# Weights in 28 to 32 KiB runs per partition through a ring of five 32 KiB slots, with block transposes on VectorE, in a decode layer

## The chip, the cores and the metric

The kernel runs on one core of a Trainium2 chip. The metric is the device time of one execution in microseconds (us), as the median over several executions. KB and KiB are 1024 bytes here, MB a million. An execution counts as slow when it is over 1.5% above the fastest of the same kernel. Anything within 2% counts as the same. The sums below use ratios to runs of the kernel before on the same chip.

## The reference, cut to what matters

It is one decode step (one token) of a transformer layer for a batch of 4: layer norm, attention over the last 2048 cached keys (32 query heads, 4 key/value heads, head size 128), output projection, residual, layer norm, a SwiGLU block with 3584 hidden units, residual.

```python
x  = A_x                                          # [4, 1, 1024]
q  = layernorm(x) @ wq                            # wq [1024, 4096]
p  = softmax(q . k[:, :, -2048:] * 128**-0.5)     # k, v: [4, 4, 8192, 128]
h  = x + (p . v[:, :, -2048:]) @ wo               # wo [4096, 1024]
n  = layernorm(h)
h2 = h + (silu(n @ w1) * (n @ w3)) @ w2           # w1, w3 [1024, 3584], w2 [3584, 1024]
```

Everything is bf16. The inputs that must be read once come to 55.58 MB: wq, k, v and wo are 8.39 MB each, and w1, w3, w2 are 7.34 MB each. There are only four tokens, so each weight is used very little: this is a program that streams memory.

## The kernel before

All large inputs pass through one ring of ten slots of 16 KiB per partition, in the order wq, k, v, wo, w1, w3, w2. A slot is refilled when the matmuls that read it are done. How a weight is laid over the 128 partitions sets how many contiguous bytes (a run) go to one partition in one DMA.

```python
stream = ctx.enter_context(tc.tile_pool(name="stream", bufs=10))
...
wq_v = A_wq.rearrange("(p kc) n -> p kc n", kc=KC)             # 2 rows = 16 KB per run
wo_v = A_wo.rearrange("(h4 p r) n -> p h4 r n", p=P, r=RPO)    # 4 rows =  8 KB per run
w2_v = B_w2.rearrange("(j p i) n -> p j i n", p=P, i=IF)       # 7 rows = 14 KB per run
...
    in_=(B_w1, B_w3)[i][c * KPC * P : (c + 1) * KPC * P, :].rearrange("(p r) f -> p r f", r=KPC)  # 14 KB
...
    in_=A_v_cache[b, :, Sk - W : Sk, :].rearrange("g (p j) d -> p g j d", j=NK)   # v: 4 KB per run
```

K is read in 16 KB runs. The layout of a weight also fixes where the activations that meet it must stand. So the kernel before turns them with PE (TensorE, the matrix engine; here a matmul against the identity or a selection matrix) and copies the result out of PSUM, the memory that matmuls write to:

```python
for r in range(RPO):                     # attention output, for wo
    nc.tensor.matmul(o4_ps[:, r, :, :, :], lhsT=sel[:, r, :, :], rhs=OT_sb[:], start=True, stop=True)
for hh in range(RPO):
    nc.vector.tensor_copy(out=o4[hh * MP : (hh + 1) * MP, :, :, :]..., in_=o4_ps[hh * MP : ...])
...
for i in range(IF):                      # SwiGLU product, for w2
    nc.tensor.transpose(out=hg_ps[:, i, :], in_=hg_v[:, i, :], identity=ident[:])
nc.vector.tensor_copy(out=hgT[:, :, :, :, 0], in_=hg_ps[:]...)
```

Of the kernel before, what the change touches and what calls it, by code (L numbers as in the profile page):

```python
# [10 lines left out]
P = 128  # L11
# [3 lines left out]
BF16 = mybir.dt.bfloat16  # L15
# [4 lines left out]
def kernel(  # L20
# [38 lines left out]
    stream = ctx.enter_context(tc.tile_pool(name="stream", bufs=10))  # L59
# [8 lines left out]
    QD = P // JG  # L68
    CQ = Hq * Dh // JG
# [3 lines left out]
    IF = CF // P  # L73
    PK = P // Hkv
    JK = W // PK
    assert CQ == REP * Dh and CF == IF * P and HF <= 512


    KPC = 2
    HPC = 8  # L80
    RPO = 4
    assert CG == KPC * P
    wq_v = A_wq.rearrange("(p kc) n -> p kc n", kc=KC)
    wo_v = A_wo.rearrange("(h4 p r) n -> p h4 r n", p=P, r=RPO)
    w2_v = B_w2.rearrange("(j p i) n -> p j i n", p=P, i=IF)

    def load_wq(c):
        wq_t = stream.tile([P, KPC, Hq * Dh], BF16, tag="s")
        nc.sync.dma_start(out=wq_t[:], in_=wq_v[:, c * KPC : (c + 1) * KPC, :])
        return wq_t  # L90

    def load_k(b):

        k_t = stream.tile([P, JK * Dh], BF16, tag="s")
        nc.sync.dma_start(
            out=k_t[:],
            in_=A_k_cache[b, :, Sk - W : Sk, :].rearrange("g (pp j) d -> pp g (j d)", pp=PK),
        )
        return k_t

    def load_v(b):
        v_t = stream.tile([P, Hkv, NK, Dh], BF16, tag="s")
        nc.sync.dma_start(
            out=v_t[:],
            in_=A_v_cache[b, :, Sk - W : Sk, :].rearrange("g (p j) d -> p g j d", j=NK),
        )
        return v_t

    def load_wo(c):
        wo_t = stream.tile([P, HPC // RPO, RPO, D], BF16, tag="s")  # L110
        nc.sync.dma_start(
            out=wo_t[:], in_=wo_v[:, c * (HPC // RPO) : (c + 1) * (HPC // RPO), :, :]
        )
        return wo_t

    def load_w13(i, c):
        w13_t = stream.tile([P, KPC, F], BF16, tag="s")
        nc.sync.dma_start(
            out=w13_t[:],
            in_=(B_w1, B_w3)[i][c * KPC * P : (c + 1) * KPC * P, :].rearrange(  # L120
                "(p r) f -> p r f", r=KPC
            ),
        )
        return w13_t

    def load_w2(j, pieces):
        w2_t = stream.tile([P, IF, D], BF16, tag="s")
        i = 0
        for n in pieces:
            nc.sync.dma_start(out=w2_t[:, i : i + n, :], in_=w2_v[:, j, i : i + n, :])  # L130
            i += n
        return w2_t

    plan = (
        [("wq", load_wq, (c,)) for c in range(KC // KPC)]
        + [("k", load_k, (b,)) for b in range(B)]
        + [("v", load_v, (b,)) for b in range(B)]
        + [("wo", load_wo, (c,)) for c in range(Hq // HPC)]
        + [("w1", load_w13, (0, c)) for c in range(KC // KPC)]
        + [("w3", load_w13, (1, c)) for c in range(KC // KPC)]  # L140
        + [("w2", load_w2, (j, [IF] if j < JG - 1 else [4, 2, 1])) for j in range(JG)]
    )
# [3 lines left out]
    def load_next(n=1):  # L146
        for _ in range(n):
            if cursor[0] < len(plan):
                kind, f, args = plan[cursor[0]]
                loaded.setdefault(kind, []).append(f(*args))  # L150
                cursor[0] += 1
# [3 lines left out]
    load_next(10)  # L155
# [8 lines left out]
    for j in range(JG):  # L164
        nc.scalar.dma_start(
            out=x_q[QD * j : QD * j + B, :], in_=x_flat[:, j * CG : (j + 1) * CG]
        )
# [20 lines left out]
    for kc in range(KC):  # L188
# [9 lines left out]
    nc.vector.memset(qz[:], 0.0)  # L198

    RS = QD // B  # L200
    spread = const.tile([P, JG, B, RS], FP32)
    nc.vector.memset(spread[:], 0.0)
    nc.vector.tensor_copy(
        out=spread[:, :, :, 0], in_=ident[:].rearrange("p (j x) -> p j x", j=JG)[:, :, :B]
    )
    hgT = act.tile([P, IF, JG, B, RS], BF16)
    nc.gpsimd.memset(hgT[:], 0.0)

    sel = const.tile([P, RPO, RPO, P // RPO], BF16)
    ident_r = ident[:].rearrange("p (m r) -> p r m", r=RPO)  # L210
    for hh in range(RPO):
        nc.vector.tensor_copy(out=sel[:, :, hh, :], in_=ident_r)
# [12 lines left out]
    for kc in range(KC):  # L225
        wq_t = loaded["wq"][kc // KPC]
        for hf in range(CQ // 512):
            for g in range(JG):
# [4 lines left out]
                    rhs=wq_t[:, kc % KPC, c0 : c0 + 512],  # L233
# [3 lines left out]
        if kc % KPC == KPC - 1:  # L237
            load_next()
# [33 lines left out]
    for u, (b, n) in enumerate(units):  # L272
        k_v = loaded["k"][b][:].rearrange("p (j d) -> p j d", d=Dh)
# [15 lines left out]
        if n == NSB - 1:  # L289
            load_next()  # L290
# [35 lines left out]
    for b in range(B):  # L326
# [10 lines left out]
        load_next()  # L337
    OT_sb = act.tile([P, Hq, B], BF16)
    nc.vector.tensor_copy(out=OT_sb[:].rearrange("p h b -> p b h"), in_=OT_ps[:])

    o4_ps = psA.tile([P, RPO, Hq // RPO, RPO, B], FP32, tag="kt3")
    for r in range(RPO):
        nc.tensor.matmul(o4_ps[:, r, :, :, :], lhsT=sel[:, r, :, :], rhs=OT_sb[:], start=True, stop=True)
    o4 = act.tile([P, Hq // RPO, RPO, B], BF16)
    MP = P // RPO
# [16 lines left out]
    for h4 in range(Hq // RPO):  # L362
# [10 lines left out]
        if h4 % (HPC // RPO) == HPC // RPO - 1:  # L373
            load_next()
# [124 lines left out]
```

## Time and profile before

| | before |
|---|---|
| time, median of the first three runs | 139.99 us |
| span in the profile | 138.0 us |
| busy: PE, VectorE (DVE), ScalarE (ACT) | 53%, 27%, 21% |
| data queue q1: bytes, packets, share of 16 engines' span | 55.58 MB, 6388, 95.4% |

These are lines of the page of the kernel before: the span, the busy time of each engine, the DMA rows (busy tenths and GB/s in 40 slices of the span), the data queue (packets, MB, share), and the chain of waits by engine.

```profile
span 138.0 us, 2358 instructions
...
PE 73.8 (53%) x1057; PEld 44.6 (32%) x1057; DVE 37.7 (27%) x72; ACT 29.1 (21%) x28; POOL 1.5 (1%) x7
...
DMA  5999999999999999999999999999999999999940
GB/s 159 447 410 432 437 423 432 446 418 423 446 401 415 414 420 424 415 431 424 427 432 420 427 434 432 424 436 428 433 424 432 432 420 440 420 445 414 415 197 2
...
q1 hardware_dynamic: 6388, 55.58, 95.4%
...
DMA 61%; PE 22%; ACT 10%; DVE 2%; issue 2%; ACTq 0%
```
The DMA row reads 9 (90% or more) in all slices but the first and the last two, while no compute engine is busy for much over half of the span. So the 16 DMA engines set the time. The chain of waits agrees. Its end, with start, length and what it was, is this:

```profile
...
76.67 27.64 DMA w_t<-in_B_w_dram
104.33 29.25 DMA w_t<-in_B_w_dram
133.62 0.62 PE y_ps L457 x6
134.25 0.43 PE y_ps L457 x3
134.71 0.42 DVE res L467
```
At 134.25 the last four matmuls begin (the chain counts three of them). After them come one VectorE copy (0.42 us) and the output DMA.

### The profile page before, as it was taken

What the parts mean: (1) busy time and instruction counts of PE and PEld (TensorE: products, weight loads), DVE (VectorE), ACT (ScalarE), POOL (GpSimd) and SP (SyncE); (2) the same over time, 40 slices, a digit from 0 to 9 for tenths busy, and PEclk for the clock granted to TensorE, in tenths of its full rate; (3) what the DMA queues carried; (4) which work ended last, traced back from release to release, by engine and by line L of the source; (5) the groups of instructions that cost most, each with busy time, mean ns of one, the idle gap of its engine ahead of it and who ended that gap; (6) DMA issues with size and microseconds to landing.
All of it is one profiled execution on the core that took longest, in us unless ns stands there. A gap on an engine that the chain in (4) does not pass through costs nothing.

```text
span 138.0 us, 2358 instructions
## 1 busy us (share of the span) xinstructions
PE 73.8 (53%) x1057; PEld 44.6 (32%) x1057; DVE 37.7 (27%) x72; ACT 29.1 (21%) x28; POOL 1.5 (1%) x7
## 2 busy tenths in 40 slices
PE   0152354499898989600596649382244422654370
PEld 0110011296565656300586637120011110233330
DVE  6710000242342525450410171510008930310001
ACT  2200000125373737449450000000041000000000
POOL 4000000000000000000000000000000000000000
PEclk9999999999999999975555557975555555555555
DMA  5999999999999999999999999999999999999940
GB/s 159 447 410 432 437 423 432 446 418 423 446 401 415 414 420 424 415 431 424 427 432 420 427 434 432 424 436 428 433 424 432 432 420 440 420 445 414 415 197 2
DMA packets 6437, 55.74 MB, mean 404 GB/s; under 512 B 504, under 2 KB 536, under 8 KB 2844
## 3 DMA queue, kind: packets, MB, share of 16 engines
q1 hardware_dynamic: 6388, 55.58, 95.4%
q8 instruction: 8, 0.13, 0.3%
q10 hardware_dynamic: 40, 0.02, 0.1%
q14 instruction: 1, 0.01, 0.0%
HBM read 55.59 MB, written 0.01 MB: 403 GB/s over the span
## 4 chain that ended last, share of the span: by engine, by line
DMA 61%; PE 22%; ACT 10%; DVE 2%; issue 2%; ACTq 0%
DMA w_t<-in_B_w_dram 41%; DMA k_t<-in_A_k_cache_dram 14%; PE kt_ps L278 11%; DMA wq_t<-in_A_wq_dram 5%; ACT kT L284 5%; PE scores_ps L263 5%; PE OT_ps L330 4%; ACT Pm L302 3%; DVE rmax L297 2%; PE pt_ps L316 1%; ACT L302 1%; PE y_ps L457 1%; ACT PT_sb L322 0%; DVE res L467 0%; DVE Dm L309 0%
## 5 line engine op out<-in xcount | busy, mean ns | idle before, releaser
L278 PE MATMUL kt_ps<-ident,k_t 128*128 128x128 bf16 x256 | 18.8, 237 | 1.0 <-DMA k_t<-in_A_k_cache_dram 1.0
L284 ACT COPY kT<-kt_ps 128x1024 bf16<-128x1024 bf16 x16 | 15.9, 1013 | 15.4 <-PE kt_ps L278 15.4
L278 PEld LDWEIGHTS <-k_t 128*128 128x128 bf16 x256 | 16.6, 107 | 6.1 <-issue 4.9
L282 DVE COPY kT<-kt_ps 128x1024 bf16<-128x1024 bf16 x16 | 11.1, 692 | 18.5 <-PE kt_ps L278 18.5
L230 PE MATMUL q_ps<-wq_t,xnT 128*4 128x512 bf16 x64 | 7.5, 621 | 11.2 <-DMA wq_t<-in_A_wq_dram 11.2
L424 PE MATMUL u_ps<-w_t,hnT 128*4 128x448 bf16 x64 | 6.7, 567 | 10.4 <-DMA w_t<-in_B_w_dram 10.4
L424 PEld LDWEIGHTS <-hnT 128*4 128x4 bf16 x128 | 3.8, 104 | 23.9 <-issue 23.2
L263 PE MATMUL scores_ps<-kT,qz 128*32 128x512 bf16 x64 | 9.9, 610 | 3.0 <-ACT kT L284 3.0
L457 PE MATMUL y_ps<-w_t,hgT 128*32 128x256 bf16 x112 | 7.1, 414 | 6.6 <-DMA w_t<-in_B_w_dram 5.8
L424 PE MATMUL g_ps<-w_t,hnT 128*4 128x448 bf16 x64 | 5.9, 516 | 5.4 <-DMA w_t<-in_B_w_dram 5.1
L330 PE MATMUL OT_ps<-PT_sb,v_t 128*128 128x8 bf16 x256 | 7.4, 168 | 2.0 <-issue 1.8
L330 PEld LDWEIGHTS <-v_t 128*128 128x128 bf16 x256 | 7.3, 104 | 2.2 <-issue 2.1
L457 PEld LDWEIGHTS <-hgT 128*32 128x32 bf16 x112 | 4.5, 135 | 9.2 <-issue 7.3
L230 PEld LDWEIGHTS <-xnT 128*4 128x4 bf16 x64 | 2.0, 106 | 15.9 <-issue 15.5
L316 PE MATMUL pt_ps<-Dm,Pm 128*128 128x128 bf16 x16 | 1.9, 311 | 9.3 <-DVE Dm L309 9.3
L366 PE MATMUL y_ps<-wo_t,o 128*4 128x256 bf16 x128 | 5.3, 344 | 1.7 <-DVE y_ps L356 1.7
L437 DVE RECIPROCAL eg<-eg 128x896 f32<-128x896 f32 x1 | 5.8, 5752 | 0.0
L240 DVE TENSOR_SCALAR q_sb<-q_ps 128x512 bf16<-128x512 f32 x1 | 0.7, 692 | 17.1 <-PE q_ps L230 17.1
L241 ACT ACTIVATE q_sb<-q_ps 128x512 bf16<-128x512 f32 x1 | 0.6, 597 | 20.9 <-DVE q_sb L240 20.9
L316 PEld LDWEIGHTS <-Pm 128*128 128x128 bf16 x16 | 1.6, 146 | 9.8 <-ACT Pm L302 9.8
L302 ACT ACTIVATE Pm<-scores_ps,nmax 128x2048 bf16<-128x2048 f32 x1 | 4.8, 4783 | 0.0
L366 PEld LDWEIGHTS <-o 128*4 128x4 bf16 x128 | 3.5, 105 | 3.5 <-DVE y_ps L356 2.0
(74 smaller groups left out, 40.5 us busy)
## 6 DMA issues: line engine op xcount, KB each, us to landing
w_t<-in_B_w_dram SPq DMA_DIRECT2D x11, 1792.0 KB, 33.3
wq_t<-in_A_wq_dram SPq DMA_DIRECT2D x4, 2048.0 KB, 11.8
k_t<-in_A_k_cache_dram SPq DMA_DIRECT2D x4, 2048.0 KB, 19.5
v_t<-in_A_v_cache_dram SPq DMA_DIRECT2D x4, 2048.0 KB, 38.4
wo_t<-in_A_wo_dram SPq DMA_DIRECT2D x4, 2048.0 KB, 22.9
w_t<-in_B_w_dram SPq DMA_DIRECT2D x1, 1024.0 KB
w_t<-in_B_w_dram SPq DMA_DIRECT2D x1, 512.0 KB, 29.2
w_t<-in_B_w_dram SPq DMA_DIRECT2D x1, 256.0 KB
```

What stands on the lines that cost most here:

```text
L230: nc.tensor.matmul(q_ps[QD * g : QD * g + B, hf * 512 : (hf + 1) * 512], lhsT=xnT[:, kc, :], rhs=wq_t[:, kc % KPC, c0 : c0 + 512], start=( ...
L263: nc.tensor.matmul(scores_ps[QD * g : QD * (g + 1), n * 512 : (n + 1) * 512], lhsT=qz[:, b, g * QD : (g + 1) * QD], rhs=kT_v[:, g, :, :], ...
L278: nc.tensor.transpose(out=kt_ps[:, jj, :], in_=k_v[:, n * NJ + t * TB + jj, :], identity=ident[:])
L282: nc.vector.tensor_copy(out=kT[:, t * TB : (t + 1) * TB, :], in_=kt_ps[:])
L284: nc.scalar.copy(out=kT[:, t * TB : (t + 1) * TB, :], in_=kt_ps[:])
L302: nc.scalar.activation(out=Pm[:].rearrange("q (c jq) -> q jq c", jq=NSB), in_=scores_ps[:].rearrange("q (jq c) -> q jq c", jq=NSB), func=A ...
L316: nc.tensor.matmul(pt_ps[:, jj, :], lhsT=Pm[:, (jb * JPB + jj) * P : (jb * JPB + jj + 1) * P], rhs=Dm[:], start=True, stop=True)
L330: nc.tensor.matmul(OT_ps[:, b, g * REP : (g + 1) * REP], lhsT=v_t[:, g, j, :], rhs=PT_sb[:, j, g * QD + b * REP : g * QD + (b + 1) * REP], ...
L366: nc.tensor.matmul(y_ps[QD * j : QD * j + B, :], lhsT=o4[:, h4, r, :], rhs=wo_t[:, h4 % (HPC // RPO), r, j * CG : (j + 1) * CG], start=(h4 ...
L424: nc.tensor.matmul(out_ps[QD * j : QD * j + B, hf, :HF], lhsT=hnT[:, k2, r, :], rhs=w_t[:, r, c0 : c0 + HF], start=(k2 == 0 and r == 0), s ...
L437: nc.vector.reciprocal(out=eg[:], in_=eg[:])
L457: nc.tensor.matmul(y2_ps[QD * j : QD * (j + 1), :], lhsT=hgT[:, i, jf, :, :].rearrange("p b s -> p (b s)"), rhs=w2_t[:, i, j * CG : (j + 1 ...
```

## The change

The intent is fewer and longer runs: a "p-major" layout, in which partition p holds consecutive rows of a weight, gives 32 KB per run for wq and wo, 28 KB for w1 and w3, and 32 KB for w2, in five slots of 32 KiB. The first slot of wq is still filled by two pieces of 16 KB, and the last slot of w2 by pieces of 10, 8, 4 and 2 KB. The new layout puts the activations just so that a 32x32 block transpose on VectorE can turn them, in place of PE transposes and strided copies. The core of the diff, with cuts:

```diff
-    stream = ctx.enter_context(tc.tile_pool(name="stream", bufs=10))
+    stream = ctx.enter_context(tc.tile_pool(name="stream", bufs=5))
...
-    wo_v = A_wo.rearrange("(h4 p r) n -> p h4 r n", p=P, r=RPO)
-    w2_v = B_w2.rearrange("(j p i) n -> p j i n", p=P, i=IF)
+    SLOT = 16384
+    RQ = 4
+    RO = 16
+    BS = 2
+    wq_v = A_wq.rearrange("(p i) n -> p (i n)", i=KC)
+    wo_v = A_wo.rearrange("(p i) n -> p (i n)", i=IO)
+    w1_v = B_w1.rearrange("(p i) n -> p (i n)", i=KC)
+    w3_v = B_w3.rearrange("(p i) n -> p (i n)", i=KC)
+    w2_v = B_w2.rearrange("(p i) n -> p (i n)", i=IF)
+    def load_rows(src, n, r0, pieces):
+        t = stream.tile([P, SLOT], BF16, tag="s")
+        i = 0
+        for m in pieces:
+            nc.sync.dma_start(
+                out=t[:, i * n : (i + m) * n], in_=src[:, (r0 + i) * n : (r0 + i + m) * n]
+            )
+            i += m
+        return [t[:, k * n : (k + 1) * n] for k in range(i)]
...
+        [("wq", load_rows, (wq_v, N_Q, c, [2, 2] if c == 0 else [4])) for c in range(0, KC, RQ)]
...                                         # k and v: two batches share a slot, runs as before
+        + [("wo", load_rows, (wo_v, D, c, [RO])) for c in range(0, IO, RO)]
+        + [("w1", load_rows, (w1_v, N_F, c, [RQ])) for c in range(0, KC, RQ)]
+        + [("w3", load_rows, (w3_v, N_F, c, [RQ])) for c in range(0, KC, RQ)]
+        + [("w2", load_rows, (w2_v, D, 0, [16])), ("w2", load_rows, (w2_v, D, 16, [5, 4, 2, 1]))]
...
-    for r in range(RPO):
-        nc.tensor.matmul(o4_ps[:, r, :, :, :], lhsT=sel[:, r, :, :], rhs=OT_sb[:], start=True, stop=True)
-    ... (four strided copies)
+    nc.vector.transpose(out=oT[:].rearrange("p b i -> p (b i)"), in_=OT_sb[:].rearrange("p b h -> p (b h)"))
+    nc.tensor.matmul(o4_ps[:], lhsT=perm[:], rhs=oT[:], start=True, stop=True)
...
-        nc.tensor.transpose(out=hg_ps[:, i, :], in_=hg_v[:, i, :], identity=ident[:])
+    nc.vector.transpose(
+        out=hgT[:].rearrange("p i x -> p (i x)"),
+        in_=hg[:].rearrange("q s c -> q (s c)").rearrange("q (c i) -> q i c", i=IF),
+    )
```

The transposes for w1/w3 (hn) change in the same way. The memsets of three PSUM tiles go, since now all rows of them are written.

More of the change, by code (lines that the diff above doesn't have):

```diff
@@ L68 @@
     QD = P // JG
+    RS = QD // B
     CQ = Hq * Dh // JG
@@ L72 @@
     HF = CF // 2
-    IF = CF // P
+    IO = Hq * Dh // P
+    IF = F // P
     PK = P // Hkv
     JK = W // PK
-    assert CQ == REP * Dh and CF == IF * P and HF <= 512
-    KPC = 2
-    HPC = 8
-    RPO = 4
-    assert CG == KPC * P
-    wq_v = A_wq.rearrange("(p kc) n -> p kc n", kc=KC)
-    wo_v = A_wo.rearrange("(h4 p r) n -> p h4 r n", p=P, r=RPO)
-    w2_v = B_w2.rearrange("(j p i) n -> p j i n", p=P, i=IF)
-    def load_wq(c):
-        wq_t = stream.tile([P, KPC, Hq * Dh], BF16, tag="s")
-        nc.sync.dma_start(out=wq_t[:], in_=wq_v[:, c * KPC : (c + 1) * KPC, :])
-        return wq_t
@@ L92, in load_k @@
-    def load_k(b):
-        k_t = stream.tile([P, JK * Dh], BF16, tag="s")
-        nc.sync.dma_start(
-            out=k_t[:],
-            in_=A_k_cache[b, :, Sk - W : Sk, :].rearrange("g (pp j) d -> pp g (j d)", pp=PK),
-        )
-        return k_t
-    def load_v(b):
-        v_t = stream.tile([P, Hkv, NK, Dh], BF16, tag="s")
-        nc.sync.dma_start(
-            out=v_t[:],
-            in_=A_v_cache[b, :, Sk - W : Sk, :].rearrange("g (p j) d -> p g j d", j=NK),
-        )
-        return v_t
@@ L109, in load_wo @@
-    def load_wo(c):
-        wo_t = stream.tile([P, HPC // RPO, RPO, D], BF16, tag="s")
-        nc.sync.dma_start(
-            out=wo_t[:], in_=wo_v[:, c * (HPC // RPO) : (c + 1) * (HPC // RPO), :, :]
-        )
-        return wo_t
-    def load_w13(i, c):
-        w13_t = stream.tile([P, KPC, F], BF16, tag="s")
-        nc.sync.dma_start(
-            out=w13_t[:],
-            in_=(B_w1, B_w3)[i][c * KPC * P : (c + 1) * KPC * P, :].rearrange(
-                "(p r) f -> p r f", r=KPC
-            ),
-        )
-        return w13_t
@@ L126, in load_w2 @@
-    def load_w2(j, pieces):
-        w2_t = stream.tile([P, IF, D], BF16, tag="s")
-        i = 0
-        for n in pieces:
-            nc.sync.dma_start(out=w2_t[:, i : i + n, :], in_=w2_v[:, j, i : i + n, :])
-            i += n
-        return w2_t
-    plan = (
-        [("wq", load_wq, (c,)) for c in range(KC // KPC)]
-        + [("k", load_k, (b,)) for b in range(B)]
-        + [("v", load_v, (b,)) for b in range(B)]
-        + [("wo", load_wo, (c,)) for c in range(Hq // HPC)]
-        + [("w1", load_w13, (0, c)) for c in range(KC // KPC)]
-        + [("w3", load_w13, (1, c)) for c in range(KC // KPC)]
-        + [("w2", load_w2, (j, [IF] if j < JG - 1 else [4, 2, 1])) for j in range(JG)]
+    assert CQ == REP * Dh and HF <= 512 and CG == QD * KC and CF == QD * IF and IO == QD == Hq
@@ new lines, in load_k @@
+    def load_k(b):
+        t = stream.tile([P, SLOT], BF16, tag="s")
+        out = []
+        for k in range(BS):
+            v = t[:, k * JK * Dh : (k + 1) * JK * Dh]
+            nc.sync.dma_start(
+                out=v,
+                in_=A_k_cache[b + k, :, Sk - W : Sk, :].rearrange("g (pp j) d -> pp g (j d)", pp=PK),
+            )
+            out.append(v)
+        return out
+    def load_v(b):
+        t = stream.tile([P, SLOT], BF16, tag="s")
+        out = []
+        for k in range(BS):
+            v = t[:, k * JK * Dh : (k + 1) * JK * Dh].rearrange("p (g j d) -> p g j d", g=Hkv, d=Dh)
+            nc.sync.dma_start(
+                out=v,
+                in_=A_v_cache[b + k, :, Sk - W : Sk, :].rearrange("g (p j) d -> p g j d", j=NK),
+            )
+            out.append(v)
+        return out
@@ new lines @@
+    N_Q, N_F = Hq * Dh, F
+    plan = (
+        [("wq", load_rows, (wq_v, N_Q, c, [2, 2] if c == 0 else [4])) for c in range(0, KC, RQ)]
+        + [("k", load_k, (b,)) for b in range(0, B, BS)]
+        + [("v", load_v, (b,)) for b in range(0, B, BS)]
+        + [("wo", load_rows, (wo_v, D, c, [RO])) for c in range(0, IO, RO)]
+        + [("w1", load_rows, (w1_v, N_F, c, [RQ])) for c in range(0, KC, RQ)]
+        + [("w3", load_rows, (w3_v, N_F, c, [RQ])) for c in range(0, KC, RQ)]
+        + [("w2", load_rows, (w2_v, D, 0, [16])), ("w2", load_rows, (w2_v, D, 16, [5, 4, 2, 1]))]
@@ L149, in load_next @@
                 kind, f, args = plan[cursor[0]]
-                loaded.setdefault(kind, []).append(f(*args))
+                loaded.setdefault(kind, []).extend(f(*args))
                 cursor[0] += 1
@@ L154 @@
     nc.scalar.dma_start(out=x_sb[:], in_=x_flat)
-    load_next(10)
+    load_next(5)
     ident = const.tile([P, P], BF16)
@@ L165 @@
         nc.scalar.dma_start(
-            out=x_q[QD * j : QD * j + B, :], in_=x_flat[:, j * CG : (j + 1) * CG]
+            out=x_q[QD * j : QD * (j + 1) : RS, :], in_=x_flat[:, j * CG : (j + 1) * CG]
         )
@@ L198 @@
     nc.vector.memset(qz[:], 0.0)
-    RS = QD // B
-    spread = const.tile([P, JG, B, RS], FP32)
-    nc.vector.memset(spread[:], 0.0)
+    ident_f = const.tile([P, P], FP32)
+    nc.vector.tensor_copy(out=ident_f[:], in_=ident[:])
+    perm = const.tile([P, P], BF16)
     nc.vector.tensor_copy(
-        out=spread[:, :, :, 0], in_=ident[:].rearrange("p (j x) -> p j x", j=JG)[:, :, :B]
-    )
-    hgT = act.tile([P, IF, JG, B, RS], BF16)
-    nc.gpsimd.memset(hgT[:], 0.0)
-    sel = const.tile([P, RPO, RPO, P // RPO], BF16)
-    ident_r = ident[:].rearrange("p (m r) -> p r m", r=RPO)
-    for hh in range(RPO):
-        nc.vector.tensor_copy(out=sel[:, :, hh, :], in_=ident_r)
+        out=perm[:].rearrange("p (h dq) -> p h dq", dq=JG),
+        in_=ident[:].rearrange("p (dq h) -> p h dq", dq=JG),
+    )
+    o4 = act.tile([P, IO, B, RS], BF16)
+    nc.gpsimd.memset(o4[:], 0.0)
     same = const.tile([P, JG, QD], FP32)
@@ L225 @@
     for kc in range(KC):
-        wq_t = loaded["wq"][kc // KPC]
+        wq_t = loaded["wq"][kc]
         for hf in range(CQ // 512):
@@ L232 @@
                     lhsT=xnT[:, kc, :],
-                    rhs=wq_t[:, kc % KPC, c0 : c0 + 512],
+                    rhs=wq_t[:, c0 : c0 + 512],
                     start=(kc == 0),
@@ L236 @@
                 )
-        if kc % KPC == KPC - 1:
+        if kc % RQ == RQ - 1:
             load_next()
@@ L272 @@
     for u, (b, n) in enumerate(units):
-        k_v = loaded["k"][b][:].rearrange("p (j d) -> p j d", d=Dh)
+        k_v = loaded["k"][b].rearrange("p (j d) -> p j d", d=Dh)
         kT = ktpool.tile([P, NJ, P], BF16, tag="kT")
@@ L288 @@
             emit_scores(u - 1)
-        if n == NSB - 1:
+        if n == NSB - 1 and b % BS == BS - 1:
             load_next()
@@ L336 @@
                 )
-        load_next()
-    OT_sb = act.tile([P, Hq, B], BF16)
-    nc.vector.tensor_copy(out=OT_sb[:].rearrange("p h b -> p b h"), in_=OT_ps[:])
-    o4_ps = psA.tile([P, RPO, Hq // RPO, RPO, B], FP32, tag="kt3")
-    for r in range(RPO):
-        nc.tensor.matmul(o4_ps[:, r, :, :, :], lhsT=sel[:, r, :, :], rhs=OT_sb[:], start=True, stop=True)
-    o4 = act.tile([P, Hq // RPO, RPO, B], BF16)
-    MP = P // RPO
-    for hh in range(RPO):
-        nc.vector.tensor_copy(
-            out=o4[hh * MP : (hh + 1) * MP, :, :, :].rearrange("p h r b -> p r h b"),
-            in_=o4_ps[hh * MP : (hh + 1) * MP, :, :, hh, :],
-        )
+        if b % BS == BS - 1:
+            load_next()
+    OT_sb = act.tile([P, B, Hq], BF16)
+    nc.vector.tensor_copy(out=OT_sb[:], in_=OT_ps[:])
+    oT = act.tile([P, B, IO], BF16)
+    nc.vector.transpose(out=oT[:].rearrange("p b i -> p (b i)"), in_=OT_sb[:].rearrange("p b h -> p (b h)"))
+    o4_ps = psA.tile([P, B, IO], FP32, tag="kt3")
+    nc.tensor.matmul(o4_ps[:], lhsT=perm[:], rhs=oT[:], start=True, stop=True)
+    nc.vector.tensor_copy(out=o4[:, :, :, 0], in_=o4_ps[:].rearrange("p b i -> p i b"))
     psA_cm.__exit__(None, None, None)
@@ L355 @@
     y_ps = psB.tile([P, CG], FP32, tag="y")
-    nc.vector.memset(y_ps[:], 0.0)
     y2_ps = psB.tile([P, CG], FP32, tag="y2")
     g_ps = psB.tile([P, 2, 512], FP32, tag="g")
-    nc.vector.memset(g_ps[:], 0.0)
     u_ps = psB.tile([P, 2, 512], FP32, tag="u")
-    nc.vector.memset(u_ps[:], 0.0)
-    for h4 in range(Hq // RPO):
-        wo_t = loaded["wo"][h4 * RPO // HPC]
-        for r in range(RPO):
-            for j in range(JG):
-                nc.tensor.matmul(
-                    y_ps[QD * j : QD * j + B, :],
-                    lhsT=o4[:, h4, r, :],
-                    rhs=wo_t[:, h4 % (HPC // RPO), r, j * CG : (j + 1) * CG],
-                    start=(h4 == 0 and r == 0),
-                    stop=(h4 == Hq // RPO - 1 and r == RPO - 1),
-                )
-        if h4 % (HPC // RPO) == HPC // RPO - 1:
+    for i in range(IO):
+        for j in range(JG):
+            nc.tensor.matmul(
+                y_ps[QD * j : QD * (j + 1), :],
+                lhsT=o4[:, i, :, :].rearrange("p b s -> p (b s)"),
+                rhs=loaded["wo"][i][:, j * CG : (j + 1) * CG],
+                start=(i == 0),
+                stop=(i == IO - 1),
+            )
+        if i % RO == RO - 1:
             load_next()
@@ L400 @@
     )
-    hn_ps = psB.tile([P, KPC, P], BF16, tag="tp")
-    hn_v = hn[:].rearrange("q (p r) -> q r p", r=KPC)
-    for r in range(KPC):
-        nc.tensor.transpose(out=hn_ps[:, r, :], in_=hn_v[:, r, :], identity=ident[:])
-    hnT = act.tile([P, JG, KPC, B], BF16)
-    nc.vector.tensor_copy(
-        out=hnT[:], in_=hn_ps[:].rearrange("p r (j x) -> p j r x", j=JG)[:, :, :, :B]
-    )
-    nc.tensor.matmul(
-        y2_ps[:], lhsT=spread[:].rearrange("p j b s -> p (j b s)"), rhs=h1[:],
-        start=True, stop=False, skip_group_check=True,
-    )
+    hnT = act.tile([P, KC, QD], BF16)
+    nc.vector.transpose(
+        out=hnT[:].rearrange("p k x -> p (k x)"), in_=hn[:].rearrange("q (c k) -> q k c", k=KC)
+    )
+    nc.tensor.matmul(y2_ps[:], lhsT=ident_f[:], rhs=h1[:], start=True, stop=False, skip_group_check=True)
     def gate_up(kind, out_ps):
-        for k2 in range(KC // KPC):
-            w_t = loaded[kind][k2]
-            for r in range(KPC):
-                for hf in range(2):
-                    for j in range(JG):
-                        c0 = j * CF + hf * HF
-                        nc.tensor.matmul(
-                            out_ps[QD * j : QD * j + B, hf, :HF],
-                            lhsT=hnT[:, k2, r, :],
-                            rhs=w_t[:, r, c0 : c0 + HF],
-                            start=(k2 == 0 and r == 0),
-                            stop=(k2 == KC // KPC - 1 and r == KPC - 1),
-                        )
-            load_next()
+        for k in range(KC):
+            for hf in range(2):
+                for j in range(JG):
+                    c0 = j * CF + hf * HF
+                    nc.tensor.matmul(
+                        out_ps[QD * j : QD * (j + 1), hf, :HF],
+                        lhsT=hnT[:, k, :],
+                        rhs=loaded[kind][k][:, c0 : c0 + HF],
+                        start=(k == 0),
+                        stop=(k == KC - 1),
+                    )
+            if k % RQ == RQ - 1:
+                load_next()
     gate_up("w1", g_ps)
@@ L442 @@
     nc.vector.tensor_tensor(out=hg[:], in0=u_ps[:, :, :HF], in1=gs[:], op=ALU.mult)
-    hg_ps = psB.tile([P, IF, P], BF16, tag="tp")
-    hg_v = hg[:].rearrange("q s c -> q (s c)").rearrange("q (p i) -> q i p", i=IF)
-    for i in range(IF):
-        nc.tensor.transpose(out=hg_ps[:, i, :], in_=hg_v[:, i, :], identity=ident[:])
-    nc.vector.tensor_copy(
-        out=hgT[:, :, :, :, 0], in_=hg_ps[:].rearrange("p i (j x) -> p i j x", j=JG)[:, :, :, :B]
-    )
-    for jf in range(JG):
-        w2_t = loaded["w2"][jf]
-        for i in range(IF):
-            for j in range(JG):
-                nc.tensor.matmul(
-                    y2_ps[QD * j : QD * (j + 1), :],
-                    lhsT=hgT[:, i, jf, :, :].rearrange("p b s -> p (b s)"),
-                    rhs=w2_t[:, i, j * CG : (j + 1) * CG],
-                    start=False,
-                    stop=(jf == JG - 1 and i == IF - 1),
-                    skip_group_check=True,
-                )
+    hgT = act.tile([P, IF, QD], BF16)
+    nc.vector.transpose(
+        out=hgT[:].rearrange("p i x -> p (i x)"),
+        in_=hg[:].rearrange("q s c -> q (s c)").rearrange("q (c i) -> q i c", i=IF),
+    )
+    for i in range(IF):
+        for j in range(JG):
+            nc.tensor.matmul(
+                y2_ps[QD * j : QD * (j + 1), :],
+                lhsT=hgT[:, i, :],
+                rhs=loaded["w2"][i][:, j * CG : (j + 1) * CG],
+                start=False,
+                stop=(i == IF - 1),
+                skip_group_check=True,
+            )
     res = act.tile([P, CG], BF16)
```

## The prediction

> **What bounds the kernel now.** The loads. The page's DMA queue lines give queue q1 55.58 MB in 6388 packets and 95.4% of 16 engines' span (131.7 of 138.0 us); in the 40 slices DMA reads 9 from the second slice to the end, about 425 GB/s. PE is busy 53%, DVE 27%, ACT 21%. The chain of waits is 61% DMA, and its last 57 us are w1/w3/w2 transfers: last landing 133.58, then 1.1 us of matmuls, 0.42 us of DVE, and the output DMA. The PE/ACT stretch of the chain (K transposes to OT, 27.6 to 76.7 us) is not the bound: DMA stays full behind it.
>
> **What the change does, costed.** The trace's DMA packet records have one size per contiguous run: 2 KB 84 ns, 4 KB 159, 8 KB 309, 14 KB 535, 16 KB 611. That is about 9 ns plus bytes/27.2 per ns. [...] By the fit (estimates) a 32 KB packet takes 1213 ns, 28 KB 1063, 10 KB 385. Per engine: wq 19.55 to 19.48 us, wo 19.78 to 19.41, w1+w3 34.24 to 34.02, w2 17.26 to 17.20. Sum: 0.7 us less DMA time. K and V are unchanged.
>
> Removed compute: four o copies (1.19 us), selection matmuls, y/g/u memsets (2.1 us), hg and hn transposes through PE with their copies. Added: three DVE block transposes (128, 256, 896 columns[...]). OT to first wo matmul (78.4 to 81.2) should fall from 2.8 to about 1.6 us. All of it hides behind the DMA.
>
> Moved: loads wait for 32 KiB slots. Capacity is the same 160 KiB, look-ahead four slots of 9.7 us instead of nine of 4.85. The second wq slot lands whole, so PE has 32 q matmuls after it (3.8 instead of 1.9 us), and K work starts about 1.3 us later. When each slot is freed, against when the queue would run dry (estimates from landings): first w1 slot issued near 59, needed by 81; second near 74, by 90; w3 near 79 and 84, by 98 and 107; w2 near 87 and 94, by 115 and 125. Never dry. The tail: w2's last pieces of 5, 4, 2, 1 rows end as before with four matmuls after the last landing; 16 rows (64 matmuls at 60 ns, 3.9 us) fit in the 7.2 us before. hgT is ready about 4 us before the first w2 slot lands.
>
> The larger pitch of the weight rows (56 or 64 KB per partition) could hurt HBM; [...] Here wq already has 64 KB pitch and runs at 431 GB/s, so I expect none.
>
> **Predicted:** 139.2 us, 8 in 10 within 138.3 to 140.2. Faster by over 2%: 0.05; within 2%: 0.90; slower by over 2%: 0.05.
>
> **What would show it.** q1 near 4,700 packets, sizes up to 32 KB at about 1213 ns; DMA 9 in all slices; wo and w1/w3/w2 phases at 430 to 435 GB/s instead of 418 to 433; last landing near 132.8; the same four-matmul tail.
>
> **What would make it wrong.** A gap in the DMA slices, where a slot is freed too late; 32 KB runs split or slower than the fit; HBM slower at the new pitch (would show as longer packets); a block transpose with strided input of several us, which would put hgT behind the w2 landing.

## More of the kernel before

Next, three stretches of the kernel before in the windows view. The columns are the stretch, its length, the busy time (and count) of each engine, the granted clock, the DMA share and the rate. The first stretch is V (4 KB runs), the second wo (8 KB), the third mostly w1 and w3 (14 KB).

```profile
core 0: us, PE busy (x) PEld busy (x) DVE busy (x) ACT busy (x) POOL busy (x), PEclk, DMA share, GB/s
43.00:60.00 17.00, 13.08 (x164) 8.44 (x163) 7.57 (x9) 8.10 (x9) 0.00 (x0) 1.00 1.02 418
64.00:79.00 15.00, 9.21 (x274) 8.99 (x275) 2.25 (x5) 5.05 (x5) 0.00 (x0) 0.50 1.01 427
84.00:114.00 30.00, 14.27 (x198) 5.76 (x191) 10.05 (x14) 2.50 (x3) 0.00 (x0) 0.61 1.01 430
...
```

The rate grows with the run: 418, 427, 430 GB/s. The DMA share is the summed duration of the packet records divided by 16 engines' time. It is 1.01 to 1.02, over 1.

## The result, and the profile after

The changed kernel took 139.39 us (median of 6 runs, 139.26 to 139.57), the kernel before 139.88 us in the same comparison (6 runs). The ratio is 0.9965, with an interval from 0.9952 to 0.9978. It is the mean time of the one kernel's fast runs over that of the other's of the same rounds, so not quite the ratio of the medians. The change is a gain of 0.49 us (139.88 x 0.0035), clear of noise, and far within "the same" at 2%. Five rounds more, later, gave 0.9967. The prediction was 139.2, within 138.3 to 140.2. That range holds the time of the kernel before as well (139.88), so that the number alone says little about the mechanism; the experiments have to show that.

The same lines of the page, of the changed kernel:

```profile
span 137.4 us, 2307 instructions
...
PE 71.2 (52%) x1045; PEld 45.2 (33%) x1045; DVE 36.3 (26%) x63; ACT 29.0 (21%) x28; POOL 1.6 (1%) x7
...
DMA  5999999999999999999999999999999999998950
GB/s 155 444 402 520 391 391 444 420 429 444 405 440 392 421 421 414 423 495 476 401 391 424 453 428 397 459 467 401 409 459 439 426 409 430 448 458 359 420 217 2
...
q1 hardware_dynamic: 4724, 55.58, 95.4%
...
DMA 70%; PE 19%; ACT 6%; SPq 1%; DVE 1%; issue 1%; ACTq 0%
```
The packets of q1 fell from 6388 to 4724: 96 data packets fewer on each of the 16 engines, and 8 packets of 4 bytes (9 ns each by the records), one for each of the 8 DMAs fewer. The share of the span is 95.4% as before, of a span that is 0.6 us shorter. The end of the chain of waits of the changed kernel:

```profile
...
94.70 0.42 SPq L97
...
95.17 37.81 DMA t<-in_B_w_dram
133.02 1.04 PE y_ps L428 x9
134.09 0.42 DVE res L438
```
Here the chain merges the matmuls of the two-row piece with the last four, since the view sees no gap between them. The timeline of PE's weight loads (PEld) of the same run shows the last four apart:

```profile
...
133.64 0.11 PEld L428 LDWEIGHTS <-hgT 128*32 128x32 bf16 x3 [0.30 <-issue]
...
```
The landing of the two-row piece moved from 133.58 to 132.98 us and that of the one-row piece, the last, from 134.21 to 133.59 (semaphore records). What follows is the same four matmuls and the same copy, which begins at 134.09 in place of 134.71. So the gain is DMA time; the tail gave nothing. Here the chain passes through the queue's issue instruction (SPq): the last slot of w2 was issued at 94.7 us, when w1's first slot came free. Its 37.81 us to landing are spent behind other loads in a full queue, so this step is no evidence that the ring held anything up. The run with four slots below tests that.

The three stretches again, in the changed kernel, with the same columns (V still 4 KB runs, wo 32 KB, w1/w3 28 KB):

```profile
...
43.00:60.00 17.00, 11.38 (x143) 7.19 (x140) 7.55 (x10) 9.32 (x10) 0.00 (x0) 1.00 1.03 421
64.00:79.00 15.00, 10.27 (x293) 9.62 (x297) 3.13 (x7) 3.10 (x5) 0.00 (x0) 0.50 0.98 419
84.00:114.00 30.00, 13.36 (x144) 6.70 (x136) 10.51 (x14) 2.50 (x3) 0.00 (x0) 0.60 1.01 434
...
```
w1 and w3 went from 430 to 434 GB/s. The wo stretch reads 419. Its bytes are counted in lumps of 32 KB, so a stretch of 15 us that begins just at the change from V to wo can't be read to 2%. In the packet records each packet's bytes can be spread evenly over its duration. Counted so, the fastest stretches of 2 MiB ran at 433.5 GB/s with 32 KB runs (wq and wo) and at 428.0 with 8 KB runs (wo of the kernel before). All of wo took 19.55 us where it had taken 19.76, w1 and w3 34.14 where 34.28, w2 without its last half MiB 15.84 where 15.95, and wq gained 0.01: about 0.48 us together.

The compute chain changed as intended. VectorE's timeline of the kernel before, for the four strided copies between attention and wo (L347) and the last copy before w2 (L448), with start and length first:

```profile
...
79.51 1.19 DVE L347 CAST o<-o_ps 32x128 bf16<-32x128 f32 x4 [0.68 <-PE o_ps L343]
...
120.99 0.65 DVE L448 COPY hgT<-hg_ps 128x112 bf16<-128x112 bf16 x1 [1.05 <-PE hg_ps L447]
...
```
and of the changed kernel, with the three block transposes (L335, L386, L420):

```profile
...
76.65 0.31 DVE L335 STREAM_TRANSPOSE oT<-OT_sb 128x128 bf16<-128x128 bf16 x1
77.34 0.72 DVE L338 CAST o<-o_ps 128x128 bf16<-128x128 f32 x1 [0.38 <-PE o_ps L337]
...
90.05 0.63 DVE L386 STREAM_TRANSPOSE hnT<-hn 128x256 bf16<-128x256 bf16 x1
...
120.88 1.70 DVE L420 STREAM_TRANSPOSE hgT<-hg 128x896 bf16<-128x896 bf16 x1
...
```
From the first copy to the first wo matmul the way is now 1.80 us (76.32 to 78.12) where it was 2.83 (78.39 to 81.22). None of this moved the end, since the loads behind it land when they land.

### The profile page after: what moved, and what is told of

Its sections match the earlier page's. It is cut to its first block, busy times and chain, and to the rows that moved or that the text cites. A ratio compares the mean times of both kernels' runs of the same rounds, so it can differ in the third digit from the quotient of the medians.

```text
span 137.4 us, 2307 instructions
## 1 busy us (share of the span) xinstructions
PE 71.2 (52%) x1045; PEld 45.2 (33%) x1045; DVE 36.3 (26%) x63; ACT 29.0 (21%) x28; POOL 1.6 (1%) x7
## 3 DMA queue, kind: packets, MB, share of 16 engines
q1 hardware_dynamic: 4724, 55.58, 95.4%
## 4 chain that ended last, share of the span: by engine, by line
DMA 70%; PE 19%; ACT 6%; SPq 1%; DVE 1%; issue 1%; ACTq 0%
DMA t<-in_B_w_dram 54%; DMA t<-in_A_wq_dram 15%; PE kt_ps L270 9%; ACT kT L276 5%; PE scores_ps L255 5%; PE q_ps L222 3%; PE g_ps L398 2%; SPq L97 1%; PE y_ps L428 1%; DVE q_sb L232 1%; ACT q_sb L233 0%; DVE res L438 0%; PE qt_ps L236 0%; ACTq L276 0%
## 5 line engine op out<-in xcount | busy, mean ns | idle before, releaser
L270 PE MATMUL kt_ps<-ident,t 128*128 128x128 bf16 x256 | 16.5, 219 | 0.0
L270 PEld LDWEIGHTS <-t 128*128 128x128 bf16 x256 | 14.4, 98 | 5.0 <-issue 4.9
L398 PEld LDWEIGHTS <-hnT 128*32 128x32 bf16 x128 | 5.5, 140 | 25.0 <-issue 22.7
L222 PE MATMUL q_ps<-t,xnT 128*4 128x512 bf16 x64 | 7.2, 615 | 12.0 <-DMA t<-in_A_wq_dram 12.0
L398 PE MATMUL u_ps<-t,hnT 128*32 128x448 bf16 x64 | 6.4, 576 | 10.6 <-DMA t<-in_B_w_dram 10.6
L428 PE MATMUL y_ps<-t,hgT 128*32 128x256 bf16 x112 | 6.7, 415 | 7.6 <-DMA t<-in_B_w_dram 7.6
L398 PE MATMUL g_ps<-t,hnT 128*32 128x448 bf16 x64 | 6.3, 574 | 8.0 <-DMA t<-in_B_w_dram 8.0
L322 PE MATMUL OT_ps<-PT_sb,t 128*128 128x8 bf16 x256 | 7.4, 168 | 1.9 <-issue 1.7
L349 PE MATMUL y_ps<-t,o 128*32 128x256 bf16 x128 | 7.2, 418 | 1.7 <-DMA t<-in_A_wo_dram 0.9
L322 PEld LDWEIGHTS <-t 128*128 128x128 bf16 x256 | 7.3, 104 | 2.1 <-issue 2.0
L349 PEld LDWEIGHTS <-o 128*32 128x32 bf16 x128 | 5.1, 144 | 3.5 <-issue 1.2
```

The costliest lines, as they stand in the source:

```text
L222: nc.tensor.matmul(q_ps[QD * g : QD * g + B, hf * 512 : (hf + 1) * 512], lhsT=xnT[:, kc, :], rhs=wq_t[:, c0 : c0 + 512], start=(kc == 0), ...
L270: nc.tensor.transpose(out=kt_ps[:, jj, :], in_=k_v[:, n * NJ + t * TB + jj, :], identity=ident[:])
L322: nc.tensor.matmul(OT_ps[:, b, g * REP : (g + 1) * REP], lhsT=v_t[:, g, j, :], rhs=PT_sb[:, j, g * QD + b * REP : g * QD + (b + 1) * REP], ...
L349: nc.tensor.matmul(y_ps[QD * j : QD * (j + 1), :], lhsT=o4[:, i, :, :].rearrange("p b s -> p (b s)"), rhs=loaded["wo"][i][:, j * CG : (j + ...
L398: nc.tensor.matmul(out_ps[QD * j : QD * (j + 1), hf, :HF], lhsT=hnT[:, k, :], rhs=loaded[kind][k][:, c0 : c0 + HF], start=(k == 0), stop=( ...
L428: nc.tensor.matmul(y2_ps[QD * j : QD * (j + 1), :], lhsT=hgT[:, i, :], rhs=loaded["w2"][i][:, j * CG : (j + 1) * CG], start=False, stop=(i ...
```

## The experiments

The theory A to test: the gain is the fixed cost of packets, of which there are fewer. The rivals: B, a loss per DMA, of which there are also fewer (22 loads on the queue where there were 30); C, the shorter compute chain; D, the ring with coarser slots gives or costs something. Twelve runs of ten kernels were made, the changed kernel being one of them, all with correct results.

| run | what differs from the changed kernel | packets per engine against it | median us | ratio to before |
|---|---|---|---|---|
| changed kernel again | nothing | 0 | 139.43 | 0.9967 |
| half runs | runs of 14 to 16 KB | +64 | 139.64 | 0.9984 |
| ten slots | the ring and the DMA sizes of before | +64 | 139.70 | 0.9988 |
| two DMAs by rows | half runs, and 8 DMAs more | +64 | 139.76 | 0.9991 |
| one-row runs | wo 2 KB, w1 and w3 7 KB | +336 | 140.91 | 1.0074 |
| kernel before | | +96 | 139.88 | 1 |
| four slots | 128 KiB ring | 0 | 139.36, 139.34 | 0.9962, 0.9961 |
| three slots | 96 KiB ring | 0 | 142.80 | 1.0194 |
| transposes twice | 2.6 us more VectorE | 0 | 139.42 | 0.9968 |
| two DMAs by partitions | halves of 64 partitions | 0 | 231.96 | 1.6585 |
| V in 16 KB runs, four slots | V's layout | -96 | 138.56, 138.57 | 0.9909, 0.9908 |

The intervals are about 0.0013 to 0.0017 wide on either side (0.2 us), except for three slots (0.0043) and partition halves (0.0030). The 139.88 of the kernel before is that of the first call; it was 139.83 to 139.96 in the others.

### The changed kernel again

> The changed kernel once more, beside the next three on the same chip and with five rounds, so that differences of 0.3% can be told. Expected 0.9965 of the kernel before, within 0.0015. Every theory expects this.

It gave 0.9967 (0.9955 to 0.998). This is the partner of the differences below.

### Half runs: only the runs put back

```diff
+    def load_pair(kind, src, n, r0, h, st):
+        # one DMA per slot, of two runs of h rows that lie st rows apart in memory
+        t = stream.tile([P, SLOT], BF16, tag="s")
+        v = src[:].rearrange("p (a x) -> p a x", a=src.shape[1] // (st * n))[:, r0 // st : r0 // st + 2, ...]
+        nc.sync.dma_start(out=t[:, : 2 * h * n].rearrange("p (a x) -> p a x", a=2), in_=v)
...
-        + [("wo", load_rows, (wo_v, D, c, [RO])) for c in range(0, IO, RO)]
+        + [("wo", load_pair, ("wo", wo_v, D, c, 8, 16)) for c in (0, 8)]
```

The loops take the rows in the new order. wq, w1, w3 and w2's first slot are done alike.

> The changed kernel with the runs alone put back to about half: each 32 KiB slot of wq (second), wo, w1, w3, w2 (first) is still filled by one DMA, but from two runs of 14 or 16 KB. Slots, number of DMAs and compute stay. Theory A (the gain is the fixed cost of about 9 ns per packet): 64 more packets per engine, 0.54 us more packet time by the sizes' medians, so about 139.9 us, ratio to before 0.999 to 1.001. Rival B (the gain is from fewer DMAs) and rival C (the gain is from the shorter compute chain): 139.4, ratio 0.9965.

It took 139.64 us, ratio 0.9984 (0.9972 to 0.9997). Against the changed kernel this is 0.24 us (139.88 x 0.0017): half of the gain was lost with the runs alone, so B and C can't explain all of it. But theory A in its form of 9 ns per packet had said 0.54 us. The sign was right and the size was not.

### Ten slots: the ring of before, the rest of the change kept

```diff
-    stream = ... bufs=5        SLOT = 16384   RQ = 4   RO = 16   BS = 2
+    stream = ... bufs=10       SLOT = 8192    RQ = 2   RO = 8    BS = 1
-        + [("w2", load_rows, (w2_v, D, 0, [16])), ("w2", load_rows, (w2_v, D, 16, [5, 4, 2, 1]))]
+        + [("w2", load_rows, (w2_v, D, 0, [8])), ("w2", load_rows, (w2_v, D, 8, [8]))]
+        + [("w2", load_rows, (w2_v, D, 16, [5])), ("w2", load_rows, (w2_v, D, 21, [4, 2, 1]))]
```

> The changed kernel with the ring of before: ten slots of 16 KiB, runs of 14 to 16 KB, DMAs one per slot (24 of weights and caches for loads, as fine as before), but the new p-major layout and the VectorE transposes kept. Theory A: packets nearly as in the half-runs kernel, so about 139.9, ratio 0.999 to 1.001, and a K phase that starts earlier changes nothing. Rival C (compute chain): 139.4. A theory that the five coarse slots cost time would expect it below the half-runs kernel, by 0.2 us or more.

It took 139.70 us, ratio 0.9988 (0.9975 to 1.0), the same as half runs within the interval. So the size of the slots has no effect that these runs can see (D). This kernel has the whole compute part of the change, but in the number of packets it differs from the kernel before in wo alone (16 KB for 8 KB, 32 packets fewer per engine). It is 0.17 us faster than the kernel before, which leaves little or nothing for C.

### Two DMAs each, by partitions: a test that tested something else

To double the DMAs and leave the packets alone, each weight DMA was cut at partition 64:

```diff
+            for p0 in (0, P // 2):
+                nc.sync.dma_start(
+                    out=t[p0 : p0 + P // 2, i * n : (i + m) * n],
+                    in_=src[p0 : p0 + P // 2, (r0 + i) * n : (r0 + i + m) * n],
+                )
```

> The changed kernel with every weight DMA cut in two by partitions (0 to 63, 64 to 127): same packets and same runs, 12 DMAs more. Theory A: 12 more semaphore packets of 9 ns per engine, 0.1 us; about 139.5, ratio 0.997. Rival B (a loss per DMA; 7 DMAs fewer would then have given 0.5 us, 0.07 us each): 0.84 us more, about 140.2, ratio 1.002.

(By the traces it is 14 DMAs more here, 37 against 23 that the queue issued, and the change had saved 8, not 7.) It took 231.96 us. Neither theory had this. The windows view of this run, with the columns of before: wq in halves, then K whole, then wo to w3 in halves.

```profile
...
10.00:40.00 30.00, 3.75 (x32) 0.87 (x32) 0.00 (x0) 0.00 (x0) 0.00 (x0) 1.00 1.05 218
46.00:60.00 14.00, 12.01 (x159) 8.01 (x152) 5.83 (x9) 7.25 (x8) 0.00 (x0) 1.00 1.01 430
100.00:190.00 90.00, 20.41 (x289) 11.30 (x286) 11.84 (x17) 2.50 (x3) 0.00 (x0) 0.50 1.00 210
...
```
All 16 engines are busy (share 1.00 to 1.05), but the weights come at 218 and 210 GB/s, while K, which still goes to 128 partitions in one DMA, comes at 430. Each 32 KB packet lasts 2548 ns (median) in place of 1213. So a weight's two halves, queued one behind the other, came at half of the rate of whole DMAs. Why they do is not shown by these runs. The prediction wasn't about this; but the run told nothing about the cost of a DMA, so that was tried again in another way.

### Two DMAs each, by rows

```diff
-    [2, 2] if c == 0 else [4]     [RO]     [RQ]     [16]
+    [2, 2]                        [8, 8]   [2, 2]   [8, 8]      # pieces of wq, wo, w1/w3, w2
```

> The number of DMAs by itself[...]: the changed kernel's five slots, each weight DMA cut in two by rows of the slot (two DMAs of half the run). Its packets are the very ones of the half-runs kernel (64 more per engine than the changed kernel), its DMAs 8 more than there. Theory A (packets only): as the half-runs kernel, 139.64 to 139.7, ratio 0.9984 to 0.999. Rival B (0.07 us per DMA): 0.56 us more than the half-runs kernel, 140.2, ratio 1.0024.

It took 139.76 us, ratio 0.9991 (0.9979 to 1.0004). Against half runs, with equal packets and eight DMAs fewer, that is 0.1 us more (0.0007 x 139.88), about 0.012 us per DMA and within the noise. B had asked for 0.56 us. With a full queue, a DMA more or less costs next to nothing here, at sizes of 1.75 to 2 MiB, which the cut ones have.

### One-row runs: the packet cost magnified

```diff
+    def load_every(kind, src, n, r0):
+        # one DMA per slot: every other row, so that each run is one row
+        v = src[:].rearrange("p (a x) -> p a x", a=k)[:, :, r0 * n : (r0 + 1) * n]
+        nc.sync.dma_start(out=t[:, : k * n].rearrange("p (a x) -> p a x", a=k), in_=v)
...
+        + [("wo", load_every, ("wo", wo_v, D, c)) for c in (0, 1)]
+        + [("w1", load_every, ("w1", w1_v, N_F, c)) for c in (0, 1)]      # w3 alike
```

> The changed kernel with one-row runs for wo (2 KB) and w1, w3 (7 KB): each slot takes every other row, still one DMA per slot. A magnified dose of the packet cost. Theory A (9 ns a packet): wo 256 packets of 84 ns per engine in place of 16 of 1213, 2.1 us more; w1 and w3 128 packets of about 273 ns in place of 32 of 1062, 0.9 us more; together 3.0 us, about 142.4, ratio 1.018. If packets cost nothing by themselves: 139.4, ratio 0.9967.

It took 140.91 us, ratio 1.0074 (1.0059 to 1.0089). Against the changed kernel that is 1.50 us (0.0107 x 139.88) for 336 packets more per engine, so 4.5 ns per packet. The form "9 ns" had said 3.0 us. Again about half. The windows view of this run, its first two stretches (V 4 KB, wo 2 KB), shows why:

```profile
...
43.00:60.00 17.00, 11.38 (x143) 7.19 (x140) 7.54 (x10) 9.32 (x10) 0.00 (x0) 0.93 1.02 420
64.00:79.00 15.00, 10.28 (x293) 9.63 (x297) 3.13 (x7) 3.11 (x5) 0.00 (x0) 0.50 1.05 407
...
```
In the wo stretch the DMA share is 1.05. Sixteen engines can't be busy for more than all of the time, so the records of an engine's neighbouring packets must overlap: the next begins a few ns before the last one ends. (The records don't name the engine, but the distances between their starts pile up at 80 ns for 2 KB and at 1209 for 32 KB, where the durations are 84 and 1213.) Duration divided by share is the pitch at which packets really follow each other. For 2 KB it is 84 / 1.05 = 80 ns; for 4 KB (V, share 1.02 to 1.03) 159 / 1.02 = 156 ns. From the rates of stretches of 2 MiB of one size, the pitch is 80 ns at 2 KB (409 to 411 GB/s), 155.5 at 4 KB (421.5), 608 at 16 KB (431.2) and 1209 at 32 KB (433.5). This is 27.2 bytes per ns plus about 5 ns per packet at all four sizes. The prediction had put a fit through the durations (84, 159, 309, 535, 611 ns) and had got 9 ns. Some 4 ns of these lie under the packet before. Whether the 5 ns arise in the DMA engine or in the memory was not tested: in all these runs a packet is a contiguous run, so the two can't be told apart.

With 5 ns, 96 packets fewer per engine give 0.48 us, where 0.49 and 0.46 were measured; 64 give 0.32, where 0.24, 0.29 and 0.34 were measured.

### Four slots, three slots: what the ring is worth

```diff
-    stream = ... bufs=5        load_next(5)
+    stream = ... bufs=4 (3)    load_next(4) (3)
```

> The changed kernel with four slots of 32 KiB in place of five (128 KiB of ring). By the same sum that the prediction used (when each slot is freed against when the queue runs dry) the tightest reuse is that of the first v slot, freed near 74 and needed by 81.6: never dry, so 139.4, ratio 0.9967, no change. A theory that the coarse ring costs look-ahead expects it slower, by 1 us or more.

> The changed kernel with three slots of 32 KiB. By the same sum the second wo slot waits for the first v slot, freed near 73.5, while the queue is dry by about 72, and the first w1 slot waits for the second v slot: first gap in the DMA. Expected slower by 2 to 6 us, 141.5 to 145.5, with a gap in the DMA slices between 60 and 80 us.

Four slots took 139.36 us (0.9962, 0.9947 to 0.9977): no change, as the sum of slot releases said. Three slots took 142.80 us (1.0194, 1.0151 to 1.0237), 3.4 us more than with four. The DMA rows of the page of the run with three slots show the gap that the sum had placed between 60 and 80 us (a slice is 3.5 us, so slices 21 and 22 are 70 to 77 us):

```profile
...
DMA  5999998999999999999957999999999999999950
GB/s 151 448 416 480 447 447 372 419 414 438 438 404 409 424 425 410 425 475 447 447 172 307 442 420 391 432 464 407 399 456 445 399 424 476 391 438 402 414 222 2
...
```
and the queue's timeline shows the second wo slot and the first w1 slot being issued only when the matmuls of V freed the slots:

```profile
...
72.65 0.34 SPq L97 DMA_DIRECT2D t<-in_A_wo_dram  x1
76.06 0.33 SPq L97 DMA_DIRECT2D t<-in_B_w_dram  x1
...
```
So four slots are enough and the fifth is spare. The second time with four slots belongs to the last experiment:

> The four-slot kernel once more, as the partner of the next run on the same chip. Expected as before: ratio 0.9965, within 0.001.

It gave 139.34 us, ratio 0.9961 (0.9947 to 0.9974).

### The block transposes done twice: is the compute chain behind the loads?

```diff
     nc.vector.transpose(out=hgT[:]..., in_=hg[:]...)
+    nc.vector.transpose(out=hgT[:]..., in_=hg[:]...)     # and so for oT and hnT
```

> The changed kernel with each of the three VectorE block transposes done twice (2.6 us more of VectorE in the chain: 0.31, 0.63, 1.70). The trace of the changed kernel has hgT ready 3.6 us before the first w2 slot lands, and the others hidden behind loads. Theory A (all compute is behind the DMA): 139.4, ratio 0.9967, no change within 0.15%. Rival C (the compute chain sets the end): up to 2.6 us more, ratio 1.015.

It took 139.42 us, ratio 0.9968 (0.9952 to 0.9985): nothing. VectorE's timeline of this run has both transposes for w2, ready at 124.34 us (122.64 + 1.70):

```profile
...
120.91 1.70 DVE L424 STREAM_TRANSPOSE hgT<-hg 128x896 bf16<-128x896 bf16 x1
122.64 1.70 DVE L428 STREAM_TRANSPOSE hgT<-hg 128x896 bf16<-128x896 bf16 x1
...
```
and PE's timeline of the same run has the first w2 matmul at 126.22, waiting for the load and not for the transpose:

```profile
...
126.22 4.67 PE L436 MATMUL y_ps<-t,hgT 128*32 128x256 bf16 x84 [6.49 <-DMA t<-in_B_w_dram]
...
```
C has fallen: 2.6 us more of it cost nothing.

### V in 16 KB runs: a version that beats both

If a packet costs 5 ns, what remains is V: 128 packets of 4 KB per engine. V can't have longer runs with all 128 partitions on one head's tokens. It can if the partitions hold (token group, kv head), as for K. Then a matmul over the partitions mixes four heads, so P must be zero where the query's head isn't the partition's. The four-slot ring gave the 16 KiB for it.

```diff
-                in_=A_v_cache[b + k, ...].rearrange("g (p j) d -> p g j d", j=NK),
+                in_=A_v_cache[b + k, ...].rearrange("g (pp j) d -> pp g (j d)", pp=PK),
...
+    for nb in range(NK):                   # spread P transposed over (pp g), 16 matmuls
+        nc.tensor.matmul(px_ps[:], lhsT=rep[:, jx, :, :]..., rhs=PT_sb[:, bb * JPB : (bb + 1) * JPB, :], ...)
+        nc.vector.tensor_tensor(out=o, in0=px_ps[:], in1=keep[:]..., op=ALU.mult)   # zero the other heads
...
-                    OT_ps[:, b, g * REP : (g + 1) * REP], lhsT=v_t[:, g, j, :], rhs=PT_sb[...]   # N = 8
+                OT_ps[:, b, :], lhsT=v_t[:, j * Dh : (j + 1) * Dh], rhs=PX[...]                  # N = 32
```

Six of the sixteen evictions go to ScalarE, with a scale per partition as the mask. It was run with four slots alone.

> An attempt to beat both: the changed kernel with four slots, and V read in 16 KB runs like K (partition = token group and kv head) in place of 4 KB runs. P is transposed as before, then spread by 16 selection matmuls over the partitions of all heads, and its eviction zeroes the other heads' part; V is then multiplied against 32 columns in place of 8. 96 packets fewer per engine. By the cost per packet that the runs so far show (4.9 ns from rates in stretches of one size, not the 9 ns of the records' durations): 0.45 us less, about 138.95, ratio 0.9935. By the 9 ns of the prediction: 0.8 us less, 138.6, ratio 0.991. The extra work (some 8 us between softmax and V) is expected to stay behind the DMA, but tightly: the first v slot is freed near 79 to 80 us and needed by 81.6; if it comes late, a gap in the DMA near 82 us eats the gain.

> The kernel with V in 16 KB runs once more, to narrow what V's runs are worth against four slots alone. At 4.9 ns for each of 96 packets per engine: 0.47 us under the four-slot kernel, ratio 0.9931. If the first result stands (0.8 us under): ratio 0.9908, and 4 KB packets cost more than the rates in stretches of one size say.

The extra work did stay behind the DMA, whose row of this run's page reads 9 from the second slice to the 38th. By PE's timelines V's first matmul came 8.62 us after the first transpose of P (62.19 to 70.81) where it came 1.69 us after it in the changed kernel (65.28 to 66.97): 6.9 us more, where the estimate was 8.

It took 138.56 us (0.9909, 0.9893 to 0.9926) and, beside four slots on the same chip, 138.57 us (0.9908, 0.9894 to 0.9921). Against four slots that is 0.74 us (0.0053 x 139.88). In the first window used above, V now runs at 428 GB/s where it ran at 421:

```profile
...
43.00:60.00 17.00, 11.00 (x136) 6.81 (x133) 7.29 (x9) 9.32 (x10) 0.00 (x0) 0.98 1.01 428
...
```
The 5 ns say 0.48 us of the 0.74, and the first form, with 9 ns, would have hit this one. The packet records say which part is which. The last data packet ended at 132.73 us in place of 133.18 with four slots, 0.45 us earlier, near the 0.48 of 96 x 5 ns; in the first profiles of the two kernels it was 0.53. More lies in the tail. The timeline of PE and its weight loads with four slots:

```profile
...
131.67 0.62 PE L428 MATMUL y_ps<-t,hgT 128*32 128x256 bf16 x16 [1.41 <-DMA t<-in_B_w_dram]
132.97 1.01 PE L428 MATMUL y_ps<-t,hgT 128*32 128x256 bf16 x12 [0.69 <-DMA t<-in_B_w_dram]
...
133.58 0.11 PEld L428 LDWEIGHTS <-hgT 128*32 128x32 bf16 x3 [0.29 <-issue]
...
```
and with V in 16 KB runs:

```profile
...
131.24 0.62 PE L461 MATMUL y_ps<-t,hgT 128*32 128x256 bf16 x16 [0.80 <-DMA t<-in_B_w_dram]
132.47 0.40 PE L461 MATMUL y_ps<-t,hgT 128*32 128x256 bf16 x8 [0.61 <-DMA t<-in_B_w_dram]
133.11 0.29 PE L461 MATMUL y_ps<-t,hgT 128*32 128x256 bf16 x4 [0.23 <-DMA t<-in_B_w_dram]
...
```
With four slots the view merges the last 12 matmuls into one row, but the weight loads show that the last four began at 133.58. So in both runs four matmuls follow the last piece, and in both the last two pieces landed about as far apart: at 132.93 and 133.54 with four slots, at 132.43 and 133.07 with V's runs (semaphore records). What differs in the tail is the granted clock of TensorE. The windows view of both runs, four slots first (columns: stretch, length, PE busy, PEclk, DMA share, GB/s):

```profile
...
132.50:134.60 2.10, 1.01 (x12) 0.60 0.16 60
...
132.50:134.60 2.10, 0.67 (x12) 0.97 0.03 10
...
```
With four slots the granted clock had fallen to 0.50 at 132.91, and from the start of the last four matmuls to the copy it took 0.45 us; with V's runs it took 0.34 us at 1.00. In the first profiles of the two kernels, both at 1.00 there, it took 0.34 us in both. So of the 0.58 us in these two traces (the last copy begins at 133.45 in place of 134.03, by VectorE's timeline) 0.47 come with the last landing and 0.11 with the clock. That V's layout has this effect on the clock is not shown. The rest of the 0.74 is within the intervals (about 0.25 us on this difference), so that the 9 ns would have come close here is no evidence for them.

## Why the prediction was right

- "What bounds the kernel now. The loads." Right. Doubling the VectorE transposes cost nothing (ratio 0.9968 against 0.9967), and the time followed the packets in all runs that moved nothing else.
- "Sum: 0.7 us less DMA time." The mechanism was right and the size was too large: 0.49 us was measured. The term that was mis-sized is the fixed cost per packet: "about 9 ns plus bytes/27.2 per ns". It is right for the duration of a record, but the records of an engine overlap by some 4 ns, and the pitch has about 5 ns. This could be read before: the windows view of the kernel before has a DMA share of 1.02 in V, and an engine can't be busy for more than all of the time. By the count above, wo gained 0.21 us where the prediction had 0.37, and w1 and w3 0.14 where it had 0.22; w2 gained 0.11 where it had 0.06, more than its 8 packets explain, and this stays open. That the predicted 139.2 was off by only 0.19 us is in part luck: it lies 0.79 below the 139.99 that it started from, 0.3 more than the gain that was measured, but the kernel before took 139.88 when measured beside the change.
- "All of it hides behind the DMA." Right, by the doubled transposes. The estimate of the transposes themselves was low: they took 0.31, 0.63 and 1.70 us. hgT was ready 3.6 us before the first w2 slot (122.58 against 126.19), where I had said about 4.
- "OT to first wo matmul ... from 2.8 to about 1.6 us." It was 1.80.
- "K work starts about 1.3 us later." Wrong, without consequence. The first K transpose began at 27.71 us where it had begun at 27.57: before, PE had been waiting for K's landing, and the later q work filled that wait.
- "Never dry." Right: four slots are as fast as five, and the slots of w1, w3 and w2 were issued at 54 to 94 us, each before the time by which it was needed. The same sum placed the gap of three slots correctly.
- "Here wq already has 64 KB pitch and runs at 431 GB/s, so I expect none." Right: wo at 64 KB pitch ran at up to 433.5 GB/s, and the 28 KB packets of w1 and w3 at 56 KB pitch took 1062 ns, as the fit had said (1063).
- "q1 near 4,700 packets" and "last landing near 132.8": 4724, and 132.98. "The same four-matmul tail" was right too: the last four matmuls begin at 134.25 and 133.63, 0.04 us after the last landing in both kernels. But what the prediction calls the last landing (133.58, and 132.8 to come) is that of the two-row piece; the last one came 0.6 us later in both.

## What to carry to other kernels

In a kernel that only streams, sum the packets per DMA engine and price each at the pitch at which packets follow each other (rate in a stretch of one size), not at the duration of its record; a DMA share above 1 in a window (1.05 with 2 KB packets here) says that records overlap. Longer runs are then worth a known and small amount: here 5 ns for each packet saved, 0.3% for 96 of the weights' 208, and the next place to look is the input with the shortest runs (V, 4 KB), not the one with the handiest layout. And before a ring is tuned, work out when each slot is freed and when the queue runs dry: it told that one slot of five was free to be spent.

## What else the traces show

- The block transposes of the changed kernel took 0.31 us for 128 contiguous columns, 0.63 us for 256 columns strided by 8 elements and 1.70 us for 896 strided by 28. That is 2.4, 2.4 and 1.9 ns per column with any fixed part. No run tells what the stride itself costs.
- The pages of both kernels list 8 packets of the instruction queue q8 (0.13 MB). Beside each, the packet records of the changed kernel show one data packet, in one place two, about 0.5 us longer than its size's median (1764 in place of 1213 ns at 79.0 us, for one), or two 4 KB packets that are 0.2 to 0.3 us longer each. What that costs the whole was not tested.
